# Block-diagonal value products, a 512-wide last-row projection, paced transfers and a new part order in a recurrent-memory transformer kernel

## The chip, the cores and the metric

The kernel runs on 1 core of a Trainium2 chip. The metric is device time in microseconds (us). An execution is also taken with a profile; durations, waits and chains below come from that one profiled execution.

## The reference

x is 2048 tokens of 512 numbers, bf16. Part A is attention with a recurrent memory, part B an MLP; both have residuals:

```
h  = x + A(layernorm(x));   out = h + B(layernorm(h))
for s in 0..63:                          # A: 64 segments of 32 tokens
    hs = concat([mem (8 rows), xs (32 rows)])
    q, k, v = hs @ Wq, hs @ Wk, hs @ Wv  # 512 -> 32 heads x 128
    p = softmax(mask(q k^T / sqrt(128))) # 40 x 40 a head
    o = concat_heads(p v) @ Wo           # 4096 -> 512
    mem = o[:8];  out_s = o[8:]
```

Rows of a segment see the memory and earlier rows of the segment. B is layernorm, 512 -> 1792, gelu, 1792 -> 512. The memory makes the segments a chain: segment s+1's q, k, v need the output projection of segment s.

## The kernel before, in words

**Rows.** A segment's 32-column tile hT holds 24 token rows ("x rows") and the 8 memory rows. The last 8 tokens of each segment are taken apart: those of four segments (a block of 128 tokens) form a tile hB, so that their q, k, v and their output projection are made once a block.

**Parts of a segment on PE**, each a list of units:
- K0, K1, Q0, Q1, V0, V1 (`passes`, L655): halves of q, k, v for hT. Each has 4 units (one for each 128 of the 512 inputs), a unit being 4 matmuls of 128x512 on four column tiles of 32 (L670; with weights kept from the unit before L423).
- SC0, SC1 (`sc_mm`, L801, matmul L815): scores of memory and last rows for half of the heads, on a mask that is copied in ahead of it (L790); `sc_softmax` (L821) makes maximum (L824), two exponentials with sums (L828), reciprocal (L831), product PC (L834) and the transposed PTC (L835). PV0, PV1 (`pv_c`, L838, matmuls L846 and L850) multiply by values; the results are copied to OT (memory rows) and OTB (last rows) at L688.
- SA (`sa_mm`, L865, L874): scores of the 24 x rows, softmax on DVE and ACT (L884 to L891), transposed to PTA (L893). PVA (`pv_a`, L896, L903): 8 x 4 matmuls of 32x24 on four row tiles; it belongs to the segment before, and `pv_a_ev` copies 768 columns to OT.
- WO (`wo`, L939, matmuls L931): output projection, 64 matmuls of 128x256; DVE transposes the result (TT, L943), then adds halves: the new memory into hT (L937, `halves_add`), and x rows into opT.
- F: the filler. In three of four segments it is k, q or v of the next block's last rows (hB); in the fourth (sg = 3) `wo_B` (L954), the projection of the last rows of the block before, 64 matmuls of 128x256, transposed to TTB (L956) and added on DVE (L959). In the last block it is the first layer of the MLP on the first 512 tokens (`w1_first`, L1064).

POOL makes the layernorm's roots, the ZC fill of the next segment (`qb_fill`, L727, L732) and copies of x^T. The values of the last rows go through HBM (`v_B_spread`, L758: 4 writes v_last, 4 reads VBD a block).

**What sets the order.** PE's order is written out: ORDER (L40) lists parts with ranges of units, the same for segments 1 to 63; START (L44) for segment 0; BANK names the PSUM banks. All other engines are ordered by a planner: `Sched.op` (L81) takes reads, writes and a planned duration, `schedule` (L160) places each operation by rank and BONUS (L28), `finalize` (L251) sets semaphore waits. SP issues nearly all transfers in one in-order queue. `align` (L305) counts PE's instructions and puts in idle weight loads (at most 8 a unit), so that each segment begins at a place PHASE (L25) modulo 256 in PE's instruction stream, unless it is only little past it.

**Start and end.** In segment 0 16 MB of weights are loaded: WV, WK, WQ, WO in a chain of transfers of 1 MB (L577 to L598). After segment 63, WK and WQ are overwritten by w1, w2 and MLP tiles; `p2_w1` (L1255) and `p2_w2t` (L1266) stream the MLP.

Of the kernel before, what the change touches and what calls it, by code (L numbers as in the profile page):

```python
# [24 lines left out]
PHASE = (87, 24, 172, 102)  # L25
KEEP = True
HALVES = ("kq", "KA", "QT", "ZCm", "VS", "nmc", "EC", "rsc", "PC", "PTC", "OTm", "KB", "QTB", "VSB")
BONUS = {"EC0": 9.64, "EC1": 2.52, "KA1": 1.19, "KB0": -4.21, "KB1": 40, "OTB": -3, "OTm0": 25.44, "OTm1": -8.14, "OTx": 40, "PA": -3.16, "PC0": 2.46, "PC1":  # L28
         4.62, "PTA": -4.05, "PTC0": -40, "PTC1": 2.94, "QT0": -2.59, "QT1": 6.99, "QTB0": 6.21, "QTB1": -0.93, "SA": -13.03, "TT": 6.79, "VBD": 1.92,
         "VS0": 0.75, "VS1": -11.93, "VSB0": -5.47, "VSB1": 15.43, "WK": 40, "WQ": 1.54, "WV": 2.9, "ZCb": 0.16, "ZCm0": 40, "ZCm1": -3.19, "ag":  # L30
         -4.83, "ag2": 40, "b1n": 6.73, "b1t": -6.81, "b2bc": 40, "cneg": -40, "gT0": 20, "hB": 3.99, "hTm": -5.4, "hTx": 5.79, "hd": -2.53, "kq0":
         4.71, "kq1": 12.67, "kq2": 10.08, "kq5": 6.67, "maskA": -7.3, "maskAF": -11.82, "maskCF": -12.78, "maskL": 40, "maskR": 2.12, "nma": -4.99,
         "nmc0": 40, "nmc1": 40, "oN": -40, "opA": 4.9, "opB": -1.91, "rs": 40, "rs2": -8.34, "rsa": -1.22, "rsc0": -3.89, "rsc1": -3.1, "sma": -4.13,
         "st2": -40, "vd": -1.71, "xT": 0.29, "xn": -10, "xr": 3.08}
# [5 lines left out]
ORDER = (("PVA", 0, 99), ("Q0", 0, 4), ("K0", 0, 4), ("Q1", 0, 4), ("K1", 0, 4), ("SC0", 0, 99), ("V0", 0, 4), ("V1", 0, 2), ("SC1", 0, 99), ("SA", 0, 99),  # L40
         ("V1", 2, 4), ("F0", 0, 2), ("PV0", 0, 99), ("F0", 2, 4), ("PV1", 0, 99), ("WO", 0, 8), ("F1", 0, 4))
BANK = dict(K0=7, K1=5, Q0=6, Q1=4, V0=6, V1=4, F0=6, F1=7, FB=5, SC0=0, SC1=1, SA=7, WO=4)
OPEN_BANK = dict(K0=4, K1=5, Q0=6, Q1=7, V0=5, V1=4, SC0=6, SC1=7, SA=5, WO=4)
START = (("B", "V", 0, (0, 6), (1, 7)), "V", "X", ("B", "V", 1, (0, 6), (1, 7)), ("B", "K", 0, (0, 4), (1, 6)), "K0", "K1", ("B", "K", 1, (0, 4), (1, 6)),  # L44
         ("B", "Q", 0, (0, 5)), "Q0", ("B", "Q", 0, (1, 4)), "Q1", "Z", "SC0", "SC1", ("B", "Q", 1, (0, 5)), "PV0", "PV1", "SA", "WO", ("T", "WO", 0, 4),
         ("B", "Q", 1, (1, 6)), ("W", 7, 12), ("T", "WO", 4, 8))


class Op:
    __slots__ = ("eng", "fn", "reads", "writes", "idx", "gidx", "deps", "sig", "sigcount", "waits",  # L50
                 "tag", "pad", "held", "name", "is_dma", "dma_sem", "dur", "mode", "rank", "start", "succ", "prev", "ni", "dma_count", "alts", "kind")
# [17 lines left out]
class Sched:  # L69
# [48 lines left out]

    def either(self, alts, reads=(), writes=(), name=None, after=()):

        eng = min(alts, key=lambda k: alts[k][1])
        o = self.op(eng, alts[eng][0], reads, writes, alts[eng][1], 0, name, after)
        if len(alts) > 1:
            o.alts = alts
        return o
# [5 lines left out]
    def dma(self, fn, kb, reads=(), writes=(), after=(), name=None, eng="sp", behind=None):  # L131
# [5 lines left out]
        o.is_dma = True  # L137
        o.prev = behind
# [112 lines left out]
    def finalize(self):  # L251
        self.schedule()
        engs = ENGINES
        know = {e: {f: -1 for f in engs} for e in engs}
        dma_known = {e: set() for e in engs}
        snap, dsnap = {}, {}
        for o in self.all_ops:
# [40 lines left out]
        for e in engs:  # L298
            c = 0
# [5 lines left out]
    def align(self):  # L305

        at, seg, owed, last = FETCH_AT, 0, 0, None
        for o in self.streams["pe"]:
            same = KEEP and o.held is not None and o.held == last
# [12 lines left out]
            at += o.ni - 4 * same + (o.pad[0] if o.pad is not None else 0)  # L322

# [117 lines left out]
def build_kernel(nc, A_x, A_mem0, A_Wq, A_Wk, A_Wv, A_Wo, B_w1, B_b1, B_w2, B_b2, out):  # L441
# [3 lines left out]
    with st:  # L445
# [43 lines left out]
        PTA = sb("PTA", [P, 2, 4, 32, 2])  # L489
        hnT0 = sb("hnT0", [P, DC, 512])  # L490
# [3 lines left out]
        TTB = sb("TTB", [P, DC, 2, 32], F32)  # L494
# [20 lines left out]
        def sc_place(bank):  # L515

            return (quad[:, bank, 256:384], ("ps", bank)) if bank < 4 else (ps[bank][:, 0:128], ("ps", bank))
# [52 lines left out]
        S.op("dve", lambda e: e.memset(KALL[:], 0.0), writes=[("KA", p, r) for p in range(2) for r in range(2)] + [("KB", p, r) for p in range(2) for r in range(2)], dur=2.3)  # L570
        S.op("dve", lambda e: e.memset(OT[:], 0.0), writes=[("OTm", p, r) for p in range(2) for r in range(2)] + [("OTx", p) for p in range(2)], dur=1.0)
# [24 lines left out]
        for g in range(4):  # L596
            load(lambda e, g=g: e.dma_start(WO[:, g * 8:(g + 1) * 8, :], wo_d[:, g * 8:(g + 1) * 8, :]), 1180, [("WO", g)])
# [190 lines left out]
        def prefill(key, mask, n, o, bkey):  # L788

            S.either({"act": (lambda e: e.copy(o, mask[:]), t_act(n)), "dve": (lambda e: e.tensor_copy(o, mask[:]), t_dve(n))},  # L790
                     reads=[key], writes=[bkey])

        def mask_mm(o, bkey):

            def f(e):
                for j in range(4):
                    ins = e.matmul(o[32 * j:32 * j + 32, :], maskL[:], maskR[:].rearrange("p a b -> p (a b)"), start=True, stop=False, tile_position=(0, 32 * j), skip_group_check=True)
                return ins
            S.op("pe", f, reads=["maskL", "maskR"], writes=[bkey], dur=0.07, mode=MC, ni=8)

        def sc_mm(s, r, bank):  # L801
# [5 lines left out]
            def f(e):  # L807
                for i in range(4):
                    for j in range(4):
# [5 lines left out]
                        ins = e.matmul(o[32 * j:32 * j + 32, 64 * sl:64 * sl + 64], ZC[:, par, h, :], rhs, start=False, stop=(i == 3),  # L815
# [5 lines left out]
        def sc_softmax(s, r, bank):  # L821
            o, bkey = sc_place(bank)
            v = o.rearrange("p (a t) -> p a t", a=2)
# [548 lines left out]
```

## Time and profile before

| what | us |
|---|---|
| median of 5 runs (862.36 to 867.14) | 864.45 |
| the profiled execution | 866.51 |
| its span | 864.8 |
| stretch 0 to 57.2 (loading, segment 0): PE busy | 32.62 |
| stretch 129.3 to 705.9 (52 segments): PE / DVE / ACT / POOL busy | 551.73 / 445.97 / 408.98 / 44.94 |
| stretch 705.9 to 776.5 (last segments, MLP loads): PE busy | 62.83 |
| stretch 776.5 to 864.8 (MLP): PE busy | 85.20 |

A row of PE's waits names the line that waited, what ended the wait, total us, times, and the longest. In the chain of waits each line is a start, a length and what the end of the program hangs on there. In the timeline a line is a start, a length, engine, source line, operation, out<-in with partitions x elements, a count, and in brackets the idle time ahead with what ended it. Overlapping matmuls run into one length: the distance of two starts says what a part costs PE, the end of the last one when its result is there. Groups show "busy, mean ns | idle before".

### The profile page before, as it was taken

Reading aid. Unit: us, or ns where it says so; the run is one execution under the profiler, and the core shown is the slowest. Engines: PE = TensorE matmul, PEld = TensorE weight load, DVE = VectorE, ACT = ScalarE, POOL = GpSimd, SP = SyncE. Lnnn points to the kernel's source line nnn. Section 1 sums busy time; section 2 is a strip of 40 time slices with the busy share of each in tenths; the row PEclk is TensorE's granted clock in tenths of the full one; section 3 lists DMA queues with packets and bytes.
Section 4 is the critical chain, followed back from the end, with each engine's and each line's share of the span. In section 5 each row is a group of like instructions: output and inputs, shape, how many; then the busy total and the mean of one; then the engine's idle time right before and its main releaser. Section 6 shows DMA issues by size and latency. Waiting matters only on the chain.

```text
span 864.8 us, 50642 instructions
## 1 busy us (share of the span) xinstructions
PE 797.9 (92%) x22121; PEld 468.8 (54%) x24166; DVE 575.9 (67%) x1870; ACT 556.0 (64%) x1547; POOL 87.6 (10%) x205
## 2 busy tenths in 40 slices
PE   3688999999999999999999999999999989889998
PEld 1245555656555555555555555655565555544443
DVE  3267677878787878777878787868687766634111
ACT  2357776767676767676767677777776758822432
POOL 4021000101010101000010101000000000006200
PEclk9889999999999999999999999999999999989999
DMA  9951010110101010101010101010113130344100
GB/s 356 367 167 23 4 29 17 31 27 25 32 23 34 23 35 22 33 15 38 17 40 17 41 17 40 11 35 11 35 28 65 46 83 10 110 152 110 49 25 25
DMA packets 65937, 49.01 MB, mean 57 GB/s; under 512 B 28468, under 2 KB 62140, under 8 KB 65724
## 3 DMA queue, kind: packets, MB, share of 16 engines
q1 hardware_dynamic: 65392, 45.50, 18.0%
q8 instruction: 182, 2.98, 1.4%
q14 instruction: 31, 0.25, 0.1%
q10 hardware_dynamic: 332, 0.27, 0.1%
HBM read 31.34 MB, written 8.39 MB: 46 GB/s over the span
## 4 chain that ended last, share of the span: by engine, by line
PE 85%; DVE 6%; issue 4%; DMA 3%; ACT 2%; SPq 0%; ACTq 0%; DVEq 0%
PE ps L670 39%; PE ps L931 18%; PE ps L423 6%; PE quad L1267 6%; PE ps L1260 4%; PE quad L846 4%; PE quad L903 2%; PE quad L815 2%; PE ps L1069 2%; DVE PC L834 1%; DVE nma L884 1%; DMA WQ<-in_A_Wq_dram 1%; DVE nmc L824 1%; DMA xr<-in_A_x_dram 1%; PE ps L874 1%
## 5 line engine op out<-in xcount | busy, mean ns | idle before, releaser
L670 PE MATMUL ps<-WV,hT 128*32 128x512 bf16 x1780 | 133.8, 380 | 0.2 <-issue 0.2
L931 PE MATMUL ps<-WO,OT 128*32 128x256 bf16 x4224 | 130.4, 276 | 2.0 <-issue 2.0
L670 PE MATMUL ps<-WQ,hT 128*32 128x512 bf16 x1796 | 124.5, 383 | 2.6 <-DVE hT L937 2.5
L689 ACT ACTIVATE kq<-ps 128x512 bf16<-128x512 f32 x160 | 94.8, 593 | 46.7 <-PE ps L670 45.4
L688 ACT CAST OT<-quad 128x128 bf16<-128x128 f32 (+1 forms) x147 | 73.1, 498 | 75.0 <-PE quad L903 55.9
L688 ACT CAST kq<-ps 128x512 bf16<-128x512 f32 x160 | 93.3, 583 | 34.7 <-PE ps L670 34.2
L931 PEld LDWEIGHTS ps<-WO,OT 128*32 128x32 bf16 x4224 | 108.1, 98 | 9.9 <-issue 4.3
L670 PE MATMUL ps<-WK,hT 128*32 128x512 bf16 x1544 | 110.4, 383 | 0.0
L711 DVE STREAM_TRANSPOSE QT<-kq 128x256 f32<-128x256 f32 x128 | 57.0, 445 | 64.7 <-ACT kq L689 64.4
L828 ACT ACTIVATE EC<-quad,nmc 128x64 f32<-128x64 f32 x252 | 77.1, 311 | 13.0 <-DVE nmc L824 12.9
L711 DVE STREAM_TRANSPOSE KALL<-kq 128x256 f32<-128x256 f32 x160 | 71.3, 445 | 20.0 <-ACT kq L688 12.4
L688 ACT CAST VS<-ps 128x512 bf16<-128x512 f32 x127 | 74.1, 583 | 0.2 <-PE ps L670 0.2
L670 PEld LDWEIGHTS ps<-WK,hT 128*32 128x32 bf16 x1544 | 47.7, 97 | 42.1 <-issue 23.4
L732 POOL COPY ZC<-QTB 128x256 bf16<-128x256 bf16 x64 | 25.7, 402 | 428.0 <-PE quad L815 399.0
L670 PEld LDWEIGHTS ps<-WQ,hT 128*32 128x32 bf16 x1796 | 49.8, 95 | 34.3 <-issue 20.7
L846 PEld LDWEIGHTS quad<-PTC,VS 32*128 32x128 bf16 x2048 | 25.0, 91 | 70.6 <-ACT EC L828 26.9
L1263 ACT ACTIVATE WQ<-ps,b1t 128x512 bf16<-128x512 f32 x42 | 28.9, 688 | 51.9 <-PE ps L1260 51.9
L670 PEld LDWEIGHTS ps<-WV,hT 128*32 128x32 bf16 x1780 | 44.2, 95 | 31.3 <-issue 20.3
L668 PEld LDWEIGHTS <-hT 128*32 128x32 bf16 x3069 | 48.6, 96 | 22.4 <-DVE hT L937 1.8
L846 PE MATMUL quad<-PTC,VS 32*128 32x16 bf16 x2048 | 36.3, 168 | 20.1 <-DVE rsc L831 5.6
L423 PE MATMUL ps<-WK,hT 128*32 128x512 bf16 x504 | 52.6, 379 | 0.0
L931 PE MATMUL ps<-WO,OTB 128*32 128x256 bf16 x1024 | 40.9, 276 | 12.2 <-issue 12.2
(145 smaller groups left out, 1361.7 us busy)
## 6 DMA issues: line engine op xcount, KB each, us to landing
WV<-in_A_Wv_dram SPq DMA_DIRECT2D x4, 1024.0 KB, 9.1
WK<-in_A_Wk_dram SPq DMA_DIRECT2D x4, 1024.0 KB, 16.9
v_last<-VSB SPq DMA_DIRECT2D x64, 64.0 KB, 2.0
WQ<-in_A_Wq_dram SPq DMA_DIRECT2D x4, 1024.0 KB, 8.7
VBD<-v_last SPq DMA_DIRECT2D x64, 64.0 KB, 2.1
WO<-in_A_Wo_dram SPq DMA_DIRECT2D x4, 1024.0 KB, 12.6
WK<-in_B_w_dram SPq DMA_DIRECT2D x4, 896.0 KB, 7.4
h_mid<-xr SPq DMA_DIRECT2D x16, 128.0 KB, 1.8
```

The lines of the kernel that those rows point to most:

```text
L423: return e.add_instruction(mybir.InstMatmult(name="I-%d" % (4000000 + _kept[0]), engine=mybir.EngineType.PE, start_tensor_calc=start, stop ...
L668: e.ldweights(l, tile_position=(0, 32 * j))
L670: ins = e.matmul(o, l, m, start=(k == 0), stop=(k == DC - 1), tile_position=(0, 32 * j), skip_group_check=True)
L688: return {"act": (lambda e: e.copy(out, src), t_act(n, ps_)), "dve": (lambda e: e.tensor_copy(out, src), 0.16 + 1.042e-3 * n * fast)}
L689: return {"act": (lambda e: e.mul(out, src, scale_), t_act(n, ps_)), "dve": (lambda e: e.tensor_scalar(out, src, scale_, None, ALU.mult), ...
L711: S.op("dve", lambda e: e.transpose(out, src), reads=[("kq", i)], writes=[key], dur=t_dve(256) + 0.02)
L828: ins = e.activation(EC[:, r, sl, :], o[:, 64 * sl:64 * sl + 64], ACTF.Exp, bias=nmc[:, r, sl:sl + 1], accum_out=smc[:, r, sl:sl + 1])
L846: e.matmul(quad[:, j, (4 * r + i) * 16:(4 * r + i) * 16 + 16], VS[rows, s % 3, r, i * E:(i + 1) * E], PTC[rows, r, c0:c0 + 16, i // 2], st ...
L931: ins = e.matmul(ps[bank][32 * j:32 * j + 32, 0:256], lhs(slot(h)), wo_cols(h, b), start=(k == 0), stop=(k == 15), tile_position=(0, 32 * ...
L1260: ins = e.matmul(ps[bank][:, 0:SBT], W1[:, cc, fc * P:(fc + 1) * P], hnT_of(k)[:, cc, :], start=(cc == 0), stop=(cc == DC - 1))
L1263: S.op("act", lambda e: e.activation(gT[:, fc, :], ps[bank][:, 0:SBT], ACTF.Gelu_apprx_tanh, bias=b1t[:, fc:fc + 1], scale=1.0), reads=[(" ...
L1267: S.op("pe", lambda e: e.matmul(quad[:, t, :], gT_of(k, fc)[:, t * P:(t + 1) * P], W2[:, fc, :], start=(fc == 0), stop=(fc == FC - 1)), re ...
```

## The change

- **PVA.** The transposed probabilities PTA are copied by POOL, four copies of 32 partitions, into a block-diagonal tile BD (zeroed once at the start, two of them in turn). `pv_a` then makes 8 matmuls of 128 rows and 96 columns in place of 32 of 32 rows and 24 columns. Its results lie in other columns of the quad banks, and the scores SC move in these banks with them. It takes its place after WO.
- **Last-row projection.** `wo_B` makes 32 matmuls of 128x512 in place of 64 of 128x256. DVE transposes 512 columns; the adds of four partition quarters go to POOL in 14 operations. POOL operations on fewer than 128 partitions wait for the POOL operation before them and the next waits for them (`narrow`).
- **Paced transfers.** After planning, `windows` takes each SP transfer from segment 2 on and makes it wait for a PE operation, so that by the plan it lies between two 256-instruction borders of PE's stream (1.0 us after one, ending 0.8 us ahead of the next), unless it would come too late; SP's queue is sorted anew.
- **Order.** A new ORDER and START, other banks, PHASE and BONUS. F is now one part in quarters; for k, q, v both halves share a weight load (`two_passes`).
- **Pieces.** WO is loaded in 16 pieces, early w1 in pieces of 64 KB, w2 in 7 and w1 in 8 pieces (before: 2 and 2); hnT0 moves into x rows.

```diff
-PHASE = (87, 24, 172, 102)
+PHASE = (164, 250, 155, 235)
 KEEP = True
+WINDOWS, WIN_LO, WIN_HI = True, 1.0, -0.8
...
-ORDER = (("PVA", 0, 99), ("Q0", 0, 4), ("K0", 0, 4), ("Q1", 0, 4), ("K1", 0, 4), ("SC0", 0, 99), ("V0", 0, 4), ("V1", 0, 2), ("SC1", 0, 99), ("SA", 0, 99),
-         ("V1", 2, 4), ("F0", 0, 2), ("PV0", 0, 99), ("F0", 2, 4), ("PV1", 0, 99), ("WO", 0, 8), ("F1", 0, 4))
-BANK = dict(K0=7, K1=5, Q0=6, Q1=4, V0=6, V1=4, F0=6, F1=7, FB=5, SC0=0, SC1=1, SA=7, WO=4)
+ORDER = (("Q1", 0, 2), ("Q0", 0, 4), ("Q1", 2, 4), ("K0", 0, 4), ("K1", 0, 4), ("V0", 0, 4), ("SC0", 0, 99), ("F", 0, 1), ("SA", 0, 99), ("SC1", 0, 99), ("V1",
+         0, 4), ("F", 1, 2), ("PV0", 0, 99), ("F", 2, 3), ("PV1", 0, 99), ("WO", 0, 8), ("PVA", 0, 99), ("F", 3, 4))
+BANK = dict(K0=6, K1=4, Q0=5, Q1=7, V0=7, V1=7, F0=4, F1=6, FB=4, SC0=1, SC1=0, SA=5, WO=7)
...
-         ("B", "Q", 0, (0, 5)), "Q0", ("B", "Q", 0, (1, 4)), "Q1", "Z", "SC0", "SC1", ("B", "Q", 1, (0, 5)), "PV0", "PV1", "SA", "WO", ("T", "WO", 0, 4),
-         ("B", "Q", 1, (1, 6)), ("W", 7, 12), ("T", "WO", 4, 8))
+         ("B", "Q", 0, (0, 5)), "Q0", ("B", "Q", 0, (1, 4)), "Q1", "Z", "SC0", "SC1", ("B", "Q", 1, (0, 5)), "PV0", "PV1", "SA", "WO", ("T", "WO", 0, 3),
+         ("B", "Q", 1, (1, 6)), ("T", "WO", 3, 5), ("W", 7, 4), ("T", "WO", 5, 6), ("W", 7, 4), ("T", "WO", 6, 7), ("W", 7, 4), ("T", "WO", 7, 8))
...
+    def narrow(self, o):
+        o.mode = 9
+        return o
...
+        o.span = 0.2 + kb / 300.0
...
+        self.wire()
+        if WINDOWS:
+            self.windows()
+            self.wire()
+
+    def windows(self):
+
+        self.align()
+        pe = self.streams["pe"]
+        ends = [o.start + o.dur for o in pe]
+        t0 = min(o.start for o in pe if o.tag is not None and o.tag[0] == 2)
+        marks = [t for t in self.marks if t > t0] + [1e9]
+        used = [m + WIN_LO for m in marks]
+        for o in self.streams["sp"]:
+            early = o.start
+            for d in o.deps:
+                early = max(early, d.start + d.dur + self.lat(d, o))
+            o.start = early
+            if not o.is_dma or o.start < t0:
+                continue
+            late = min([d.start - o.dur - 2.0 for d in o.succ], default=1e9)
+            size = o.span
+            w = max(0, bisect.bisect_right(marks, early) - 1)
+            while w < len(marks) - 1:
+                t = max(early, used[w])
+                if t + size <= marks[w + 1] + WIN_HI or t > late:
+                    break
+                w += 1
+            if w >= len(marks) - 1 or t > late:
+                continue
+            used[w] = t + size
+            i = bisect.bisect_right(ends, t) - 1
+            o.start = max(t, ends[i])
+            if pe[i] not in o.deps:
+                o.deps.append(pe[i])
+        self.order()
...
+        for a, b in zip(self.streams["pool"], self.streams["pool"][1:]):
+            if (a.mode == 9 or b.mode == 9) and not a.is_dma and a not in b.deps:
+                b.deps.append(a)
...
+            if at // FETCH_N > was:
+                self.marks.append(o.start + o.dur / 2)
...
-        PTA = sb("PTA", [P, 2, 4, 32, 2])
-        hnT0 = sb("hnT0", [P, DC, 512])
+        PTA = sb("PTA", [P, 4, 32, 2])
+        BD = sb("BD", [P, 2, 4, 4, NA, 2])
...
-            return (quad[:, bank, 256:384], ("ps", bank)) if bank < 4 else (ps[bank][:, 0:128], ("ps", bank))
+            w = quad[:, bank, :].rearrange("p (a n) -> p a n", a=2)[:, :, 128:192] if bank < 4 else ps[bank][:, 0:128].rearrange("p (a n) -> p a n", a=2)
+            return w, ("ps", bank)
...
-        for g in range(4):
-            load(lambda e, g=g: e.dma_start(WO[:, g * 8:(g + 1) * 8, :], wo_d[:, g * 8:(g + 1) * 8, :]), 1180, [("WO", g)])
+
+        def quarter(v, q):
+            return v.rearrange("p (r a k) d -> p r a k d", r=2, a=2)[:, q // 4, :, 2 * (q % 4):2 * (q % 4) + 2, :]
+        for q in range(8):
+            for a in range(2):
+                load(lambda e, q=q, a=a: e.dma_start(quarter(WO[:], q)[:, a], quarter(wo_d, q)[:, a]), 295, [("WO", q, a)])
...
-            S.op("dve", lambda e: e.transpose(PTA[:, par].rearrange("p a t b -> p (a t b)").bitcast(F32), PA[:].rearrange("p a t b -> p (a t b)").bitcast(F32)),
-                 reads=["PA"], writes=[("PTA", par)], dur=0.31)
+            S.op("dve", lambda e: e.transpose(PTA[:].rearrange("p a t b -> p (a t b)").bitcast(F32), PA[:].rearrange("p a t b -> p (a t b)").bitcast(F32)),
+                 reads=["PA"], writes=["PTA"], dur=0.31)
+            for j in range(4):
+                rows = slice(32 * j, 32 * j + 32)
+                S.narrow(S.op("pool", lambda e, j=j, rows=rows: e.tensor_copy(BD[rows, par, :, j, :, :], PTA[rows, :, 0:NA, :]), reads=["PTA"], writes=[("BD", par, j)], dur=0.56))
...
-                    for j in range(4):
-                        rows = slice(32 * j, 32 * j + 32)
-                        ins = e.matmul(quad[:, j, 256 + 24 * k:280 + 24 * k], VS[rows, par, k // 4, (k % 4) * E:(k % 4 + 1) * E], PTA[rows, s % 2, k // 2, 0:NA, k % 2],
-                                       start=(s == NS - 1 and k == 0), stop=True, tile_position=(32 * j, 0), skip_group_check=True)
+                    ins = e.matmul(rows_a(k), VS[:, par, k // 4, (k % 4) * E:(k % 4 + 1) * E], BD[:, s % 2, k // 2, :, :, k % 2],
+                                   start=(s == NS - 1 and k % 2 == 0), stop=True, skip_group_check=True)
                 return ins
-            S.op("pe", f, reads=[("VS", par, 0), ("VS", par, 1), ("PTA", s % 2)], writes=QK, dur=0.26, mode=MR, ni=64)
+            S.op("pe", f, reads=[("VS", par, 0), ("VS", par, 1)] + [("BD", s % 2, j) for j in range(4)], writes=QK, dur=0.45, mode=MF, ni=16)
+        def rows_a(k):
+            return quad[:, k // 2, 128 + 256 * (k % 2):224 + 256 * (k % 2)]
...
-            wo_units(lambda sl: OTB[:, bk % 2, sl, :], lambda r: [("OTB", bk % 2, sg) for sg in range(4)], bank)
-            S.op("dve", lambda e: e.transpose(TTB[:].rearrange("p c q t -> p (c q t)"), ps[bank][:, 0:256]), reads=[("ps", bank)], writes=["TTB"], dur=t_dve(256) + 0.02)
-            t5 = TTB[:].rearrange("p c q (s t) -> p c q s t", s=4)
+            for q in range(8):
+                def f(e, q=q):
+                    for j in range(4):
+                        ins = e.matmul(ps[bank][32 * j:32 * j + 32, :], OTB[:, bk % 2, slot(8 * j + q), :], WO[:, 8 * j + q, :], start=(q == 0), stop=(q == 7),
+                                       tile_position=(0, 32 * j), skip_group_check=True)
+                    return ins
+                S.op("pe", f, reads=[("WO", g, a) for g in range(8) for a in range(2)] + [("OTB", bk % 2, sg) for sg in range(4)], writes=[("ps", bank)], dur=0.215, mode=MC, ni=8)
+            S.op("dve", lambda e: e.transpose(TTB[:].rearrange("p c q t -> p (c q t)"), ps[bank][:, :]), reads=[("ps", bank)], writes=["TTB"], dur=t_dve(512) + 0.02)
             o = opT[:, bk % 2, :, :].rearrange("p c (s t) -> p c s t", s=4)[:, :, :, NA:SEG]
-            S.op("dve", lambda e: [e.tensor_tensor(o[64 * q2:64 * q2 + 64], t5[0:64, :, q2], t5[64:128, :, q2], ALU.add) for q2 in range(2)][1],
-                 reads=["TTB"], writes=[("opB", bk % 2)], dur=0.6)
+            for c in (0, 2):
+                t = TTB[:, c:c + 2]
+                S.narrow(S.op("pool", lambda e, t=t: e.tensor_copy(TTS[0:64], t[64:128]), reads=["TTB"], writes=["TTS"], dur=0.7))
+                S.narrow(S.op("pool", lambda e, t=t: e.tensor_tensor(t[0:64], t[0:64], TTS[0:64], ALU.add), reads=["TTB", "TTS"], writes=["TTB"], dur=0.7))
+                S.narrow(S.op("pool", lambda e, t=t: e.tensor_copy(TTS[0:32], t[32:64]), reads=["TTB"], writes=["TTS"], dur=0.7))
+                for q in range(4):
+                    def f(e, c=c, q=q, t=t):
+                        x, y = [v[0:32, :, q].rearrange("p c (s t) -> p c s t", s=4) for v in (t, TTS)]
+                        return e.tensor_tensor(o[32 * q:32 * q + 32, c:c + 2], x, y, ALU.add)
+                    S.narrow(S.op("pool", f, reads=["TTB", "TTS"], writes=[("opB", bk % 2)], dur=0.3))
...
+        hnT0 = xr[:, 2:6, :].rearrange("p t (c n) -> p c t n", c=DC)
...
-        pieces = []
-        for i in range(2):
-            f = slice(i * (FC // 2), (i + 1) * (FC // 2))
-            pieces.append(S.dma(lambda e, f=f: e.dma_start(W2[:, f], w2_d[:, f]), 896, writes=[("W2", i)], after=used["WK"] + pieces[-2:-1]))
+        for i in range(NP):
+            f = slice(2 * i, 2 * i + 2)
+            S.dma(lambda e, f=f: e.dma_start(W2[:, f], w2_d[:, f]), 256, writes=[("W2", i)], after=used["WK"])
         p2_load(1)
-        p2_load(0)
         for i in range(2):
             f = slice(i * (F // 2), (i + 1) * (F // 2))
-            pieces.append(S.dma(lambda e, f=f: e.dma_start(W1[:, :, f], w1_d[:, :, f]), 896, writes=[("W1", i)], after=used["WK"] + pieces[-2:-1]))
+            for c in range(DC):
+                S.dma(lambda e, f=f, c=c: e.dma_start(W1[:, c, f], w1_d[:, c, f]), 224, writes=[("W1", i, c)], after=used["WK"])
+        p2_load(0)
```

## The prediction

> **What bounds the kernel now.** I read the page first (busy shares, DMA queues), then PE's waits, then the chain of waits in the steady part, then single stretches of the timeline.
>
> ```profile
> PE 797.9 (92%) x22121; PEld 468.8 (54%) x24166; DVE 575.9 (67%) x1870; ACT 556.0 (64%) x1547; POOL 87.6 (10%) x205
> ...
> q8 instruction: 182, 2.98, 1.4%
> ```
>
> PE is the bound; no other engine is over 67%. The second line is PE's instruction stream: 182 packets of 16 KB for 22121 + 24166 = 46287 instructions, so one packet per 254. In the trace these packets never come closer than 3.33 us, and where PE is at its densest they come at 3.4 to 3.6.
>
> ```profile
> PE ps L931 <- issue: 14.2, 18, 3.4
> ...
> PE quad L846 <- issue: 4.8, 10, 1.1
> ```
>
> PE's waits (us, times, longest). "issue" is a wait that no semaphore explains. It sits where instructions are many and short: the output projection (L931) and value products (L846).
>
> ```profile
> 417.65 1.86 PE ps L931 x64
> 419.51 0.86 PE ps L670 x16
> 420.37 0.30 PE quad L903 x32
> 420.67 1.02 PE ps L670 x16
> ...
> 426.97 0.12 issue
> ...
> 428.19 1.86 PE ps L931 x64
> ...
> 437.81 0.26 issue
> ...
> 439.15 2.19 PE ps L931 x75
> 441.34 0.41 issue
> ```
>
> The chain of waits. From one WO to the next is one segment: 10.54 us here (417.65 to 428.19), then 10.96 in the segment that also holds a last-row projection, where "issue" enters twice. Over the 52 segments from 129.3 to 705.9 us the mean is 576.6/52 = 11.09. Adding up starts that come later than the usual spacing gives 23.4 us on short-instruction parts without any data wait (0.45 a segment) and some 0.2 a segment at PV0 (the first L846), which waits for softmax.
>
> ```profile
> 74.25 1.93 PE L931 MATMUL ps<-WO,OT 128*32 128x256 bf16 x64
> 76.28 0.37 PE L903 MATMUL quad<-PTA,VS 32*128 32x24 bf16 x32
> 77.20 1.06 PE L670 MATMUL ps<-WQ,hT 128*32 128x512 bf16 x16 [0.54 <-DVE hT L937]
> ```
>
> Timeline of segment 3, which has no filler: Q waits for the new memory. WO start to Q start is 77.20 - 74.25 = 2.95 us, a recurrence that no order can shorten. In the steady part PE's own work fills 3.06 (417.58 to 420.64), so today it does not wait.
>
> **The change, part by part.** My sum is against the profiled execution (866.5 us; span 864.8 and 1.7 around it). The median of the runs is 864.45, 2.05 lower; I carry that over at the end.
>
> *Value products, 8 matmuls.* Removed: 32 matmuls and 32 loads, 0.33 us from its start to that of Q (420.30 to 420.64 in the timeline), plus 0.10 for the change of array shape ahead (a part of 0.86 takes 0.97 before it). Added: 8 matmuls of 128x128 on 96 columns. The nearest row:
>
> ```profile
> 19.74 0.40 PE L623 MATMUL quad<-ident,xn 128*128 128x128 bf16 x4
> ```
>
> Four load-and-multiply pairs with 128 columns; the shortest single one lasts 0.219 us, so they are (0.40 - 0.219)/3 = 0.06 us apart. Eight with 96 columns: 0.34 us at the least (0.043 each by columns), 0.48 at most, plus 0.10 for the next change of shape: 0.44 to 0.58. I take 0.45. The Trainium skill ("TensorE: Matmul & The Clock Gate", Back-to-back issue gap) speaks against the change here: in a stream of loads and matmuls it gives about 81 ns a pair at 128 columns. That makes 8 x 0.081 + 0.10 = 0.75. The row is this chip's, so I use it, and keep 0.75 as upper end. Either way PE time rises by 0.1 to 0.4; 48 instructions go.
>
> *New order, after WO.* Now WO, PVA, one quarter of F, then Q1: 1.75 + 0.10 + 0.45 + 0.43 = 2.73, under the recurrence's 2.95. So Q1 waits 0.2 for hT, and PVA's dearer matmuls cost nothing (by the skill's figure 3.03, 0.08 over it). PVA writes all four quad banks: the copies after PV1 (0.29 and 0.38) end under WO's 1.75. Its own evacuation (ACT 0.80) comes some 5 us ahead of the next SC on those banks; uncovered it would cost 0.80. The stretch WO to Q goes from 3.06 to 2.95.
>
> *New order, Q to WO.* Today 7.48 (420.64 to 428.12), 0.18 of it wait: 7.30. Three quarters of F lie here instead of two: + 0.43. Changes of array shape are six, as now. So 7.73 + w, w being PV0's wait.
>
> ```profile
> 413.50 0.31 PE L815 MATMUL quad<-KALL,ZC 128*32 128x64 bf16 x16
> ...
> 416.55 0.27 PE L846 MATMUL quad<-PTC,VS 32*128 32x16 bf16 x16 [0.19 <-DVE rsc L831]
> ```
>
> SC0 to PV0 takes 3.05 today. In the new order PE has 0.12 + 0.43 + 0.26 + 0.12 + 0.86 + 0.43 + 0.10 = 2.32 of work between them. The bare softmax chain by its rows is 0.38 (scores, hop) + 0.29 + 0.70 (two exponentials with their sums) + 0.17 + 0.30 + 0.24 and some 0.33 of hops: 2.41. Low end w = 0.09. In the timeline 0.16 and 0.35 are lost because DVE takes the reductions of SC1 and SA ahead of this chain's product and transpose; kept whole (3.05) w = 0.73. Now SC1 ends 1.1 us after SC0's start, while ACT still runs the exponentials, so its reduction fits there: I take 2.52, w = 0.20.
>
> *Last-row projection 512 wide.* 32 matmuls of 512 for 64 of 256: the same 1.72 us of columns, 64 instructions less. DVE's transpose grows from 0.45 to about 0.7, its adds (2 x 0.29) go to POOL, 14 operations each. Nothing on PE waits for them: the rows are wanted a segment later.
>
> *POOL.* Its rows:
>
> ```profile
> L732 POOL COPY ZC<-QTB 128x256 bf16<-128x256 bf16 x64 | 25.7, 402 | 428.0 <-PE quad L815 399.0
> ```
>
> With 0.295 for 128 and 0.509 for 384 columns a 192-column copy is 0.35; four are 1.4 us a segment, 90 in all, and the adds some 100 (14 operations, about 6.6 us, 16 times). POOL goes from 88 to near 280, in order. Behind the block-diagonal copies, which wait for PTA, stands the next ZC fill, with 8 us to spare. Sharing with DVE: the PC product takes 0.40 beside a POOL copy and 0.30 without; the hT adds showed 0.19 either way. I take 0, upper end 0.2 on the recurrence.
>
> *Instruction stream.* Per four segments: 11 packets today (2816 with padding). Gone are 4 x 48 (PVA), 64 (last rows) and 3 x 16 (F shares its loads): 304, so 10 packets. More to the point is density: in a last-row segment WO, last rows and PVA are 128 + 64 + 64 = 256 instructions in 1.75 + 0.97 + 0.33 = 3.05 us, under the 3.33 between packets; the stall of 0.41 sits right there. In the new order WO to Q holds 128 + 16 + 16 in 2.95. The Trainium skill ("Runtime: NRT & Kernel Launch", Instruction fetch mechanics) says a 16 KB boundary costs a tail-bump that is mostly hidden. If so, the 0.45 is something else and stays: 10.67 + 0.20 + 0.45 = 11.32, slower than now. The rows decide for a stall: no semaphore explains it and it comes only where 256 instructions take less than a packet's spacing. I leave 0.05 (ends 0 and 0.45).
>
> *Paced transfers.* Each transfer on SP waits for a PE matmul between two packets. Behind it stand SP's other transfers, first VBD's, wanted some 17 us later; the delay is one spacing, about 4 us: 0 on PE. Without that cover PV0 would wait up to 4 us once in four segments. The gain is in the longer fetches beside big loads: the 3.35 us (the longest in the table above) at 756 us while w2 loads in pieces of 896 KB, and 1.4 us at 708. I take 4 of these 4.8. The smaller w1 and w2 pieces are wanted from 776 us on, 27 us after their room is free: 0.
>
> *Start.* WO comes in eight quarter-row pairs; after the last one 1 unit instead of 4 is left: - 0.65. The memset of BD lies under 20 us of loading: 0. hnT0 moves into x rows last used in segment 56: 0.
>
> **Sum.** Segment: 2.95 + 7.73 + 0.20 + 0.05 = 10.93 for 11.09: - 0.16 x 52 = - 8.3. End of the loop - 4.0, start - 0.7. Together - 13.0: 853.5 profiled, 851.4 against the median.
>
> **Rivals.**
> Softmax takes PV0's place as bound (slower): w = 0.73. The segment is 11.46, + 0.37 x 52 = + 19, less 4.7: 879. For it: DVE's order today loses half a microsecond. Against: SC1 now follows SC0 sooner. It decides from w = 0.45, where the segment gains nothing net of start and end. Chance 0.20.
> The stalls go only half, since the stretch from SC0 to PV1 still has some 250 instructions in 3 us: 0.22 left, the segment 11.10, the end only - 2: 862. Chance 0.17.
> Everything closes: w = 0.09, no stall, the end - 4.8: 10.77, - 17 - 5.5: 842. Chance 0.13.
> The sum as worked out: 0.50, its own range 844 to 859 (PVA by the skill's figure + 4, POOL beside the adds + 5, w within 0.1 of mine).
>
> **Numbers.** What a measurement here can tell from no change is 0.3%, 2.6 us. Faster by more: 0.50 + 0.13 + 0.03 of the half case; within: 0.13; slower: 0.21. The range, 838 to 872, leaves out most of the softmax rival's upper half and a tail below.
>
> **What would show it.** PVA's group 8 matmuls 0.45 to 0.5 us before F; Q1 with an idle of about 0.2 from DVE hT; PV0's idle from DVE or ACT about 0.2; "issue" before L931 near zero; q8 at about 165 packets; POOL near 280 us busy. Wrong if PV0 or PV1 wait over 0.45, if hT's adds stretch beside POOL, or if "issue" only moves to SC, SA and PV.

## The result, and the profile after

The changed kernel takes 859.53 us (median of 24 runs, 855.30 to 862.81), the kernel before 864.17 (43 runs). The ratio is 0.9943, 95% interval 0.9931 to 0.9956: 4.9 us faster by the ratio (the two medians are 4.6 apart). The direction was right and the time lies in the range, but I had forecast 13.

The profiled execution took 858.34, its span is 856.6 (864.8 before). Cut at the output projections (WO) of segments 7, 59 and 63, the 8.2 us between the two spans are:

| stretch | before | after | difference | forecast |
|---|---|---|---|---|
| start to WO(7) | 129.3 | 129.6 | + 0.3 | - 0.7 |
| WO(7) to WO(59), 52 segments | 576.6 | 562.0 | - 14.6 | - 8.3 |
| WO(59) to WO(63), 4 segments | 47.9 | 57.7 | + 9.8 | one stall less, within the - 4.0 |
| WO(63) to the end | 111.0 | 107.3 | - 3.7 | - 4.0 |

Before's profiled execution lies 2.05 over its median of five, that of after 1.2 under its own; so 8.2 here and 4.9 against that median.

The two lines of the page that the prediction shows of the kernel before, now of the changed one:

```profile
PE 805.2 (94%) x20073; PEld 447.8 (52%) x22282; DVE 597.3 (70%) x1782; ACT 562.5 (66%) x1609; POOL 263.8 (31%) x686
...
q8 instruction: 166, 2.72, 1.3%
```

3932 instructions of PE and 16 packets fewer, POOL three times as busy. Neither line shows what went wrong. The chain of waits in the steady part (start, length, what), for one segment:

```profile
411.05 1.86 PE ps L1009 x64
412.91 0.46 PE quad L977 x8
413.36 0.33 PE ps L744 x4
413.69 0.22 PE ps L490 x4
413.91 0.02 issue
413.93 1.92 PE ps L744 x32
...
421.73 1.86 PE ps L1009 x64
```

WO, then PVA in 0.46, a quarter of the filler, then Q 2.9 after WO; the next WO 10.7 after this one. The "issue" entries of 0.1 to 0.4 that stood before WO are gone. Most segments without a last-row projection now take 10.69, nearly to the hundredth.

In the last block it is otherwise. PE's waits from WO(59) to WO(63) (us in total, times, longest):

```profile
PE quad L919 <- ACT EC L901: 4.6, 3, 2.0
PE ps L744 <- DVE hT L1015: 4.3, 3, 1.7
PE ps L1009 <- ACT OT L762: 1.5, 2, 0.7
PE quad L919 <- DVE rsc L904: 1.4, 1, 1.4
```

11.8 us where before has 4.0. Both PV0 (L919) and the recurrence (hT) wait. The chain there, from the end of one segment into the next (L1168 is Gelu, L959 and L901 are Exp; an ACT line without a tile is a load of a function table):

```profile
718.74 1.28 ACT L1168
720.04 0.69 ACT hT L1168
720.91 0.37 ACT OTB L762
721.30 1.28 ACT L959
722.60 0.42 ACT SA L959
723.04 0.42 DVE sma L960
723.70 0.33 DVE TT L1021
...
729.69 1.28 ACT L901
730.98 0.71 ACT EC L901 x4
```

PE stands in none of the lines shown. After PE's wait of 1.98 us for EC, up to 718.09, its granted clock was 0.5 for 3.4 us, and this WO took 3.52 us for 1.86; but TT had to wait for DVE's reduction (723.04) in any case, and the three segments take 15.5, 15.6 and 14.6, so this is not what they share. ACT loads Gelu's table, does the first chunk's Gelu, loads Exp's table for SA; DVE, in order, reduces SA before it transposes WO's result (TT), so the memory is late. After a second Gelu ACT loads Exp's table again ahead of PV0. The kernel before has 8 table loads in all, this one 14. Beside one at the start of each they are, before (L1073 is Gelu, L828 the scores' Exp) and after:

```profile
L1073 ACT ACT_TABLE_LOAD x4 | 5.1, 1283 | 0.1
L828 ACT ACT_TABLE_LOAD x3 | 3.8, 1283 | 0.1
```

```profile
L1168 ACT ACT_TABLE_LOAD x7 | 9.0, 1283 | 0.1
L959 ACT ACT_TABLE_LOAD x3 | 3.8, 1283 | 0.1
L901 ACT ACT_TABLE_LOAD x3 | 3.8, 1283 | 0.1
```

### The profile page after: what moved, and what is told of

Its sections match the earlier page's. It is cut to its first block, busy times and chain, and to the rows that moved or that the text cites. A ratio compares the mean times of both kernels' runs of the same rounds, so it can differ in the third digit from the quotient of the medians.

```text
span 856.6 us, 47416 instructions
## 1 busy us (share of the span) xinstructions
PE 805.2 (94%) x20073; PEld 447.8 (52%) x22282; DVE 597.3 (70%) x1782; ACT 562.5 (66%) x1609; POOL 263.8 (31%) x686
## 4 chain that ended last, share of the span: by engine, by line
PE 85%; DVE 5%; ACT 5%; DMA 4%; issue 1%; SPq 0%; ACTq 0%; DVEq 0%
PE ps L744 38%; PE ps L1009 14%; PE ps L490 8%; PE quad L1362 5%; PE ps L1355 4%; PE quad L919 3%; PE ps L1036 3%; PE quad L977 2%; PE quad L889 2%; ACT EC L901 2%; PE ps L947 1%; DMA WQ<-in_A_Wq_dram 1%; DVE hT L1015 1%; DMA xr<-in_A_x_dram 1%; DVE TT L1021 1%
## 5 line engine op out<-in xcount | busy, mean ns | idle before, releaser
L762 ACT CAST OT<-quad 128x128 bf16<-128x128 f32 (+1 forms) x192 | 85.1, 443 | 121.0 <-PE quad L977 79.1
L970 POOL COPY BD<-PTA 32x192 bf16<-32x192 bf16 x256 | 87.7, 343 | 229.1 <-DVE PTA L966 217.2
L744 PE MATMUL ps<-WV,hT 128*32 128x512 bf16 x1780 | 121.4, 381 | 0.0
L1009 PEld LDWEIGHTS ps<-WO,OT 128*32 128x32 bf16 x4224 | 107.3, 97 | 11.2 <-issue 2.7
L763 ACT ACTIVATE kq<-ps 128x512 bf16<-128x512 f32 x146 | 80.4, 595 | 47.0 <-PE ps L744 47.0
L744 PE MATMUL ps<-WK,hT 128*32 128x512 bf16 x1544 | 108.4, 383 | 0.0
L762 ACT CAST kq<-ps 128x512 bf16<-128x512 f32 x146 | 86.2, 591 | 11.5 <-PE ps L744 6.5
L742 PEld LDWEIGHTS <-hT 128*32 128x32 bf16 x3652 | 60.7, 96 | 61.4 <-DVE hT L1015 37.9
L901 ACT ACTIVATE EC<-quad,nmc 128x64 f32<-128x64 f32 x252 | 77.1, 311 | 8.6 <-DVE nmc L897 3.2
L744 PEld LDWEIGHTS ps<-WV,hT 128*32 128x32 bf16 x1780 | 47.9, 96 | 43.3 <-issue 20.4
L785 DVE STREAM_TRANSPOSE QT<-kq 128x256 f32<-128x256 f32 x128 | 55.7, 436 | 14.6 <-ACT kq L763 10.3
L919 PEld LDWEIGHTS quad<-PTC,VS 32*128 32x128 bf16 x2048 | 24.8, 91 | 76.8 <-ACT EC L901 29.3
L744 PEld LDWEIGHTS ps<-WQ,hT 128*32 128x32 bf16 x2048 | 54.9, 95 | 19.0 <-issue 2.2
L1358 ACT ACTIVATE WQ<-ps,b1t 128x512 bf16<-128x512 f32 x42 | 28.9, 688 | 52.8 <-PE ps L1355 52.8
L960 DVE TENSOR_REDUCE sma<-SA 128x8 f32<-128x256 f32 x64 | 26.8, 420 | 44.3 <-ACT SA L959 44.2
L490 PE MATMUL ps<-WK,hT 128*32 128x512 bf16 x504 | 51.1, 379 | 0.0
```

The lines of the kernel that those rows point to most:

```text
L490: return e.add_instruction(mybir.InstMatmult(name="I-%d" % (4000000 + _kept[0]), engine=mybir.EngineType.PE, start_tensor_calc=start, stop ...
L742: e.ldweights(l, tile_position=(0, 32 * j))
L744: ins = e.matmul(o, l, m, start=(k == 0), stop=(k == DC - 1), tile_position=(0, 32 * j), skip_group_check=True)
L762: return {"act": (lambda e: e.copy(out, src), t_act(n, ps_)), "dve": (lambda e: e.tensor_copy(out, src), 0.16 + 1.042e-3 * n * fast)}
L763: return {"act": (lambda e: e.mul(out, src, scale_), t_act(n, ps_)), "dve": (lambda e: e.tensor_scalar(out, src, scale_, None, ALU.mult), ...
L785: S.op("dve", lambda e: e.transpose(out, src), reads=[("kq", i)], writes=[key], dur=t_dve(256) + 0.02)
```

## Experiments

Ratios are against runs of the kernel before on the same chip (it took 860.8 to 863.0 there). Where a step is split: WO to the first queries (Q), Q to the first scores (SC0), SC0 to PV0.

**e1: Gelu after all Exp of a segment.** In segments 60 to 62 another order:

```diff
+LAST_ORDER = (..., ("SC0", 0, 99), ("SA", 0, 99), ("SC1", 0, 99), ("V1", 0, 4), ("F", 0, 1), ("PV0", 0, 99), ("PV1", 0, 99), ("WO", 0, 8), ("PVA", 0, 99), ("F", 1, 4))
+            seq = LAST_ORDER if bk == NTB - 1 and sg < 3 else ORDER
```

> Only segments 60 to 62 change: their order on PE puts the scores of the x rows and of the second half right behind the first scores and brings the filler's first quarter (the first layer of the MLP with its Gelu) after V1, so that all Exp of a segment come before its two Gelu. Theory A (ACT goes to and fro between Exp and Gelu: 14 loads of a function table for 8, and DVE's in-order work behind an Exp waits for them): 8 loads again, the four steps from the output projection of segment 59 to that of 63 fall from 57.7 us to 48 to 50, so about 851 us (848 to 853). Theory B (the last segments wait for pieces of the MLP's weights or for normalized rows, or the new order suits them badly in itself): the four steps stay at 56 to 58 and the time at 859.

852.04 us, ratio 0.9893 (0.9864 to 0.9922). 8 table loads again; the four steps take 51.6 us, 6.0 less. So the loads are the larger part, but 3.7 us over before stayed, which theory A hadn't foreseen. The stages say where (us; typical segments):

| kernel, stretch | WO to Q | Q to SC0 | SC0 to PV0 |
|---|---|---|---|
| before, steady | 3.06 | 3.46 | 3.05 |
| before, last block | 3.17 | 3.46 | 4.04 |
| after, steady | 2.95 | 4.33 | 2.38 |
| after, last block | 5.36 | 4.33 | 4.70 |
| e1, last block | 3.65 | 5.03 | 3.79 |

From SC0 to PV0, where the load for the scores' Exp stands, before loses 1.0 over its steady 3.05 and e1 1.4 over 2.38. That the shorter stretch covers less of the load fits this; it is not shown apart, since e9 loses 1.0 there without any load. In e1 both Gelus stand before ACT's copies of k and q, and a quarter of the filler waits 0.5 us a segment for one of them.

**e2: without pacing.** `WINDOWS` is False.

> The changed kernel without the pacing of transfers. If the pacing removes stalls of PE's instruction stream beside big transfers: stalls come back at the end of the loop (up to 4.8 us) and in the steady part, 862 to 868 us. If the stalls are gone because fewer instructions come in a given time (the density theory): within 2 us of the changed kernel, 858 to 862, and no wait without a cause over 0.5 us in the steady part.

861.65 us, ratio 1.0003 (0.9987 to 1.0019): 5 us slower than the changed kernel, and no stall of the instruction stream. One segment takes 17.07 us; the others are as fast or faster (last-row segments 10.75 for 10.9 to 11.3). Its chain:

```profile
648.21 4.09 DMA xT<-h_mid
...
652.40 0.41 DVE xn L1153
...
653.70 0.32 DVE TT L1021
...
654.54 2.75 PE ps L744 x21
```

DVE stands before the normalization of a row of h that a 4.09 us transfer brings; behind it in order is TT, and with it the memory. Paced, the same load is issued 2.4 us ahead of WO and not 0.4 behind it (one VBD read goes before it on SP, not four), and DVE waits 0.73. Two windows of e2 (length, then busy time of each engine, the granted clock the first number after POOL's brackets):

```profile
650.80:654.50 3.70, 0.00 (x0) 0.01 (x2) 1.99 (x8) 0.71 (x3) 0.73 (x2) 0.79 0.02 2
654.50:658.00 3.50, 3.46 (x36) 1.84 (x112) 2.06 (x5) 0.60 (x1) 2.14 (x6) 0.50 0.00 0
```

After 3.7 idle us PE ran at clock 0.50 for 3.5 us: the segment with this 3.8 us of wait is 6.3 longer than the other last-row segments. From WO(63) to the end this kernel takes 106.5, so the 3.35 us stall beside w2 is gone without pacing too. The smaller pieces may have done that, or the missing dense place (before's stall stands just behind WO, in its last-row projection): no run has the large pieces in the new order.

**e3 and e7: the 32 row-tiled products of before, in the new place.** No BD, no copies on POOL; e7 has other places in the stream:

```diff
-                    ins = e.matmul(rows_a(k), VS[:, par, ...], BD[:, s % 2, k // 2, :, :, k % 2], ...)
+                    for j in range(4):
+                        ins = e.matmul(quad[:, j, 256 + 24 * k:280 + 24 * k], VS[rows, par, ...], PTA[rows, s % 2, ...], ...)
-PHASE = (164, 250, 155, 235)
+PHASE = (164, 58, 27, 171)        # e7 only
```

> The changed kernel with the 32 row-tiled value products of before, in the new place after the output projection, and without the block-diagonal copies on POOL. By my sum the stretch from the output projection to the first queries is bound by the recurrence at 2.95 us either way, so the product's own 0.35 or 0.45 us lie beside the wait for the memory: the segment stays at 10.8, the time within 3 us of the changed kernel (857 to 862). If 64 instructions for 16 bring the stalls of the instruction stream back: + 0.2 to 0.4 a segment, 868 to 880. If the copies on POOL slow DVE on the recurrence (a transposed memory addition of 0.22 for 0.19): - 1 to - 3 us.

> e3 again, with places of the segments in the instruction stream that suit its 48 more instructions a segment (in e3 over 60 idle loads a segment came in by misfit: 54326 instructions). If e3's 12.11 a segment was the misfit: 10.8 to 10.9 a segment, and the block-diagonal product in itself is worth about nothing, 857 to 862. If it is density (WO, 32 products and the filler are 128 + 64 + 16 instructions in 2.7 us, under the 3.33 us between two packets): 11.0 to 11.4 a segment, 867 to 890.

e3: 928.44 us, ratio 1.0787 (1.0743 to 1.0830), 12.11 a segment. e7: 899.32, 1.0413 (1.0390 to 1.0435), 11.58, also above the forecast. So the other places are worth some 30 us; e8 asks whether the rest is the 48 instructions. The dearest wait of PE in e7's steady part:

```profile
PE quad L973 <- issue: 24.4, 25, 1.5
```

L973 is the product. In two of four segments (12.3 and 12.5) it stops in the middle; the other two take 10.7 and 10.8, so the product's own 0.3 us for 0.46 are worth nothing, as I had worked out; what it loses lies in the segments with stalls.

**e8: 48 idle weight loads a segment in WO**, the work unchanged. `PHASE` is that of e7, and the alignment adds 16 idle loads a segment elsewhere.

```diff
+                    for n in range(6):
+                        e.ldweights(lhs(slot(2 * q)), tile_position=(0, 32 * (n % 4)))
```

> The changed kernel with 6 idle weight loads ahead of each unit of the output projection (48 a segment), places in the stream as in e7. The work is the same; only the number of instructions from WO to the first queries goes from 160 to 208, as in e7. Density theory: the stalls are a matter of instructions in a given time, so the segment lengthens as in e7, 11.0 to 11.4, with waits without cause at WO or PVA. If stalls come from the row-tiled form or its change of array shape: 10.8 to 10.9, while e7 is slow. The loads themselves take PE time too: each that doesn't hide behind a product adds up to 0.02 us, 0.5 us in WO at the most if half of them show.

906.58 us, ratio 1.0485 (1.0456 to 1.0514), 11.70 a segment. PE's wait, and a place in the chain:

```profile
PE ps L1011 <- issue: 29.3, 25, 1.9
```

```profile
315.52 1.67 PE ps L1011 x50
317.19 1.60 issue
318.79 0.40 PE ps L1011 x6
```

The same stall, 25 times in 52 segments, now inside WO, on products that haven't changed. Most segments without it take 10.73 to 10.75, so the loads themselves cost 0.05. The trace ties the stalls to the instruction packets: all 24 over 0.3 us at this line end 1.2 to 1.6 us after a packet has come in, and in e7 the 25 at L973 do too. Density is right, with the place of a border: two of four segments have the same 208 instructions there and no stall. The size was wrong: a stall takes 1.2 us, not 0.2 to 0.4, and the segment lies above the forecast of 11.0 to 11.4.

**e4: the order of before** (ORDER and BANK), with the new product.

> The changed kernel with the part order and banks of before; everything else (block-diagonal products, last rows 512 wide, pacing, pieces) as changed. If the order carries the steady gain (the value product lies beside the recurrence's wait only after the output projection, and the density of instructions there falls): the segment goes back to 11.1 to 11.3 us, + 14 to + 24, while the last four segments keep 8 table loads and 48 us, - 9: 864 to 875 in all. If the 512-wide projection and the fewer instructions carry it: segment 10.8 to 10.9 and last segments 48 us, so about 851.

1021.1 us, ratio 1.1847 (1.1811 to 1.1883), 13.51 a segment. At the head of a segment the product waits for the copies, and scores wait for ACT:

```profile
PE quad L889 <- ACT ZC L799: 94.4, 62, 2.8
PE quad L977 <- POOL BD L970: 58.6, 58, 3.2
```

The first is a wait of 1.5 a segment that I haven't followed further; the second is 1.0, PVA at the head of the segment waiting for the block-diagonal copies. Both guesses were too small: the new product needs a later place, and the order is part of its price. In this run the last four steps took over 14 us each, so its 8 table loads did not bring them back to 48 in all.

**e5: POOL's copies of x^T behind the memory additions**, by a dependence.

```diff
+                    S.op("pool", ..., reads=["xT"] + after, ...)     # after: [("hTm", (s + 1) % RING)]
```

> The changed kernel; the two POOL copies out of the transposed x^T (128x128 and 128x384) wait for the memory additions into hT of the segment that they fall in. Theory (in the segment after a last-row projection the additions take 0.70 us for 0.39 because these copies now run beside them, and the recurrence grows from 2.95 to 3.26): 0.3 in some 12 to 14 segments, span 852 to 853.5 for 856.6, about 4 us under the changed kernel. Rival (the additions are slow there for another reason, DVE's own queue or a transfer): additions stay at 0.70 in those segments, time within 1.5 us of the changed kernel.

857.56 us, ratio 0.9926 (0.9901 to 0.9952); span 855.4, 1.2 under the changed kernel. The reason for it, from the timelines of DVE and POOL of the changed kernel:

```profile
218.40 0.70 DVE L1015 TENSOR_TENSOR hT<-TT 64x32 bf16<-64x32 f32 x2
```

```profile
218.35 0.50 POOL L707 COPY hT<-xT 128x384 bf16<-128x384 bf16 x1
```

Beside this copy the two additions take 0.70, elsewhere mostly 0.39. In e5 they are 0.39 there, and up to 0.68 in the next segment, into which the copies slid. The additions do lose time beside the copies; a gain over the changed kernel (0.9943) is not told by the intervals, and the forecast gain of 4 was a miss.

**e6: e5, and e1 with V0 behind SC0.**

> The edit of e5 and, in segments 60 to 62, the order of e1 with V0 moved behind the first scores, so that 0.86 us more of products lie between the first scores and PV0, where ACT's table load for Exp comes. If what e1 still lost there (51.6 us in four steps for 47.9 before) is that load, no longer covered since the new order has only 2.3 us between SC0 and PV0: the four steps fall to 49 to 50. Together with e5's 4 us: span 843 to 846, some 1.9 to 2.3% under the kernel before. If Gelu ahead of the copies of k and q is what is left: 51.5 stays and the span is 846 to 847.

852.91 us, ratio 0.9877 (0.9859 to 0.9895). The four steps take 52.8: V0 between SC0 and PV0 helped nothing, since SC0 itself comes later (Q to SC0 5.06, waiting for ACT's copy of k). That leaves Gelu ahead of these copies; e9 takes it away.

**e9 and e10: Gelu after the loop.** The six chunks are copied as they are, Gelu follows in place after segment 63; in e10 ACT also makes the copies of x^T.

```diff
+            if fc < 6:
+                S.either(copy2(g[:, fc % 2, :], ps[bank][:, 0:SBT], 512), reads=[("ps", bank)], ...)
+        for fc in range(6):
+            gelu_late(fc)              # reads "PA": after the last Exp
-                S.op("pool", lambda e: e.tensor_copy(dA, ...))
+                S.op("act", lambda e: e.copy(dA, ...))               # e10 only
```

> The changed kernel and its order throughout; the first six chunks of the MLP's first layer are copied out of PSUM as they are (bf16, without bias and Gelu), and their Gelus run in place after the last Exp of segment 63, so that a single change of function table is left in the loop. Theory (all that the last block lost is Gelu: its table loads, ACT's time for them and what waits behind ACT and DVE): the four steps from segment 59's output projection to that of 63 fall to 43 to 44.5 us (57.7 in the changed kernel, 47.9 before, 51.6 in e1), since each is then a usual segment of 10.7 to 11.1. The six Gelus take 6 x 0.69 = 4.1 us after the loop, beside PE's work on the other eight chunks, at the worst on its path: span 842.5 to 846.5, 1.7 to 2.4% under the kernel before. Rival (the pieces of the MLP's weights or the normalized rows also hold the last segments up): 46 or more in the four steps, span 847 or more.

> e9, and the two copies out of the transposed x^T on ACT in place of POOL. If POOL's copies beside DVE's memory additions cost what the changed kernel shows (WO to Q of 3.07 to 3.29 in some 6 of the 14 segments after a last-row projection): another 1 to 2.5 us, span 840.5 to 845.5, and no memory addition over 0.5 us beside these copies. If ACT, at 66%, has no room for 0.8 us more there: the softmax before PV0 is late instead, and the time is that of e9 or up to 2 us above.

e9: 848.10 us, ratio 0.9833 (0.9799 to 0.9867). e10: 847.36, 0.9826 (0.9802 to 0.9850). Both beat both kernels. In e9 one table load is left after the first:

```profile
L1176 ACT ACT_TABLE_LOAD x1 | 1.3, 1283 | 0.0
```

The four steps take 45.8 (11.73, 11.71, 11.69, 10.69), 11.9 less than in the changed kernel; the six Gelus cost 0.9 after the loop (108.2 for 107.3). Three steps still lose 1.0 at PV0: the second half's reduction stands on DVE behind the first half's transpose, and the second Exp waits 1.03 for it. This I had not foreseen. e10 over e9 is nothing that the intervals tell, and the 52 steady segments take 560.5 in e9 and 560.7 in e10: no gain by moving POOL's copies is seen.

**e11 and e12: the last-row projection of before, and its control.** In both the alignment is off (`PHASE = ()`); e11 also has `wo_B` of before.

> The changed kernel with the last-row projection of before (64 matmuls of 256, adds on DVE) and no alignment of segments in the instruction stream; e12 is its control, without alignment too. Density theory: 64 more instructions in every fourth segment, in the filler that lies beside SC, SA and PV and after the value product: stalls of 0.3 to 0.6 us in these segments, 52/4 x 0.45 = 6 us over e12, 2 to 9. If DVE and POOL matter more (two adds of 0.3 us on DVE come back, 14 POOL operations go): last-row segments get shorter, at or up to 3 us under e12.

> The changed kernel without alignment in the instruction stream (no idle loads, 206 instructions less in four segments; the borders of 256 fall anywhere). If what matters is instructions in a given time: the stretch WO, PVA, filler holds 160 in 2.95 us, always under 256 in 3.33, so the time is that of the changed kernel within 2 us, with fewer stalls if anything. If the place of a border matters too: waits without cause of 0.1 to 0.4 us come in some segments, 2 to 8 us more.

e11: 860.14 us, ratio 0.9972 (0.9948 to 0.9996). e12: 859.22, 0.9960 (0.9938 to 0.9981). That the 512-wide projection gains is not shown: 1 us between the two, which the intervals don't tell from nothing. The median last-row segment is 10.7 and 10.8, and with 64 more instructions beside scores and value products the waits without cause are 4.0 us in the steady part, for 1.5 in e12: 2.5 more, within the forecast 2 to 9. Alignment shows no gain either (0.9960 without, 0.9943 with): where the dense place is gone, a border may fall anywhere.

**e13: e9's edit on the kernel before.**

> The kernel before with e9's edit alone: the six early chunks copied out of PSUM, their Gelus after the loop. If the rest of the change is worth what the steady part shows (14.6 us in 52 segments, 3.7 at the end) and only its last block hid that, then before loses little by Gelu in its loop: its four last steps go from 47.9 to 44 to 45 us and its time falls by 2 to 4 us, to 0.995 to 0.998 of before, and e9 stays 10 to 13 us ahead of it. If e9's gain is that of its edit and not of the change, before gains 9 us or more by the same edit, 0.99 or under.

859.14 us, ratio 0.9974 (0.9951 to 0.9997), the four steps 44.2. So before gains 2 us by the edit and the changed kernel 9 to 10. Without Gelu in the loop the change is worth 0.9833 / 0.9974 = 0.986 (0.982 to 0.990 by both intervals), 12 us. In the two profiles (845.8 and 857.0) the 52 steady segments are 15.1 shorter in e9, the start 3.9 longer, the last four steps 1.7 longer and the end 1.7 shorter.

## Why the forecast was right in its parts and wrong in its sum

- **WO to Q, 2.95 with PVA hidden in it**: right. PVA takes 0.46 (I took 0.45). The 81 ns a pair of the Trainium skill ("TensorE: Matmul & The Clock Gate", Back-to-back issue gap) gave an estimate of 0.75; the row of before was the better guide.
- **Q to WO, 7.73 + 0.20 + 0.05**: 7.74 measured. PV0 doesn't wait: SC0 to PV0 is 2.38 where PE's own work is 2.32. The softmax rival (w = 0.73) is out; the low end of w was the value.
- **Stalls by density**: shown by e8 and its packets, with e7; and the rule of the Trainium skill that a boundary is mostly hidden ("Runtime: NRT & Kernel Launch", Instruction fetch mechanics) doesn't hold for this stream: 25 stalls of 1.2 us come with 48 loads that do nothing. Only the place counts where 208 instructions follow each other in 3 us; in the filler 64 more did little (e11).
- **Steady segment**: 10.81 for the forecast 10.93. The 0.12 over 10.69 sit mostly in last-row segments (11.06). Part of it is the sharing of DVE and POOL that I took as 0: WO to Q was 3.07 to 3.29 in seven of 14, in three of them with additions of 0.53 to 0.70 beside the copy. Moving the copies brought no gain that the runs tell, so most of the 11.06 is not settled.
- **End of the loop, - 4.0**: - 3.7 came behind WO(63), but not from pacing (e2); smaller pieces and density were not told apart. The smaller of the two stalls I counted, at 708 us, lies ahead of WO(63) and was 1.23, not 1.4. Pacing, taken as free and as worth part of these 4, is worth 5 us for another reason, by luck: it issues one load 2.8 us earlier against WO.
- **Start, - 0.7**: + 0.3. WO(1) comes only 0.2 earlier, and the step after it takes 12.25 us for 10.42 before; why is not followed. One profile can't settle this term: with the same START the stretch took 128.5 to 131.3 in e1, e2, e5, e6, e9 and e10.
- **The step that failed**: "- 0.16 x 52 = - 8.3. End of the loop - 4.0, start - 0.7". It prices the new order in the 52 steady segments, and for the rest only transfers. In segments 60 to 62 the filler is the MLP's first layer, and the same reordering moves its Gelus: F in quarters ends its first chunk just before PV0, so that Gelu falls between the Exp of the scores and that of SA. That is four table loads a segment of 1.28 us instead of two, Gelu ahead of k's and q's copies, and, it seems, in the shorter stretch from SC0 to PV0 less cover for the load. + 9.8 us where the sum had nothing but that stall's gain. e1 shows 6.0 of it with two loads a segment again, and e9 the whole without Gelu in the loop. There the change is worth 12 us (e9 against e13). That this is near the forecast 13 is luck: the steady part gives 15 of it for the forecast 8.3, and start, last steps and end take 3.9 of that back where 4.7 were to come.

The row that would have told was in the profile of before: 8 loads of 1283 ns, four at Gelu's line and three at Exp's.

## What to carry to other kernels

When an order is changed for all rounds of a loop, walk through each kind of round, above all the last ones, where the filler is something else; a sum made from the steady part says nothing of them. On ACT count the changes of function as instructions of 1.28 us that no planner with durations alone sees, and ask what covers each. And where PE issues many short instructions, look at how many come in the time of a packet before you ask how long each takes.

## What was not expected of the hardware

- 48 idle weight loads a segment, which cost 0.05 us by themselves (with 16 of the alignment), made a segment 11.70 - 10.81 = 0.89 us longer (e8); 29.3 / 52 = 0.56 of it is the stalls of the instruction stream themselves, the rest is not split.
- After 3.7 idle us TensorE's granted clock was 0.50 for the next 3.5 us and 0.71 in the mean of the 3.0 after them (e2), so this wait cost more than its length. In the changed kernel one of two waits of 2.0 us was followed by 3.4 us at 0.5.
- DVE beside POOL, in the changed kernel: two 64x32 additions in 0.70 us for 0.39, beside a 128x384 copy.
